# One tuned attention-and-FFN kernel on one core: hidden tiles of the bias moved between engines, and VectorE's work in a late attention step put in another order

## The chip, the core and the metric

The kernel runs on one core of a Trainium2 chip. The metric is the device time of one execution in microseconds (us), as the median of several executions. The core has a matrix engine (TensorE, PE in the profile) and three engines for other work: VectorE (DVE), ScalarE (ACT) and GpSimd (POOL). SyncE (SP) issues the DMA transfers. Each engine runs its own queue of instructions in order; engines wait for each other by semaphores.

## The reference

Three stages follow each other. The first is attention with a relative bias that a tiny network makes out of the two positions, the second and third are two feed-forward networks over 1152 tokens.

```
scores = q @ k.T / sqrt(64)                       # 2 batches, 8 heads, 576 x 576, head size 64
x      = log1p(|i - j|) / log1p(max(i, 1))
bias   = relu(x * w1 + b1) @ w2                   # 32 hidden units, one column for each head
attn   = softmax(scores + bias);  out = attn @ v
h = x @ w_in;  g = h * sigmoid(1.702 h);  x = g @ w_out          # 512 -> 2048 -> 512
h = x @ w_in;  g = P(h) / (Q(h) + 1e-6);  x = g @ w_out          # P cubic, Q with |h| and h*h
```

## The kernel before

**The bias** is made in 36 beats, `i` = 0 to 35, each for 16 rows of positions. A beat `i` emits three things, in this order: `bias_out(i-3)`, which scales a finished PSUM result into the SBUF tile `st` (line L137 on ScalarE, L135 on VectorE in three beats), makes the mirrored part of it by a copy called the image (L139 ScalarE, L141 VectorE, L143 GpSimd) and stores it to DRAM; `bias_matmul(i-2)` (L117), which multiplies four hidden tiles by `w2` into a PSUM tile (`wide`, of which there are two that the attention scores also use, or `narrow`, of which there is one); and `bias_hidden(i)`, which makes the four hidden tiles of its rows, `max(u, -b)` or the same as a relu, in the buffer `room`. The tiles are 304 to 576 columns wide. Hidden tiles 0 and 1 are VectorE's (L98), tile 2 is GpSimd's (L93), tile 3 is ScalarE's (L91), but in the beats 4, 5, 6, 11, 16, 21, 24, 26, 30 and 33 it is VectorE's. VectorE reads `u` from SBUF (`bc`) where a tile is wider than 512 columns, which is so in the beats 0 to 7, and from a copy of it in PSUM (`up`) elsewhere. `room` has three buffers that the beats use in turn, two from beat 30 on.

**The attention** has 40 steps. A step handles 128 queries of two heads, or 64 queries of two heads as one block ("single-head" in VectorE's eyes: one pass over 576 columns); the latter has `qc` 4. On PE a step issues the transpose of a late piece of step s-3 (`tails`, L279, into the first scores tile), the scores of step s (L213, twelve matmuls in a two-head step, the heads in turn), some products with v (L338, L341) and the transposes of step s-3 (L306). On VectorE it issues, for each head, one instruction that adds the bias and takes the minimum (L234, followed by a short read of its accumulator), the sum plus a small number of step s-1 (L221), the reciprocal of it (L248), and the copy of the transposed late piece out of PSUM (`PTt`, L288, or two small ones, L292). ScalarE then makes the exponentials (L238). GpSimd scales the exponentials of step s-1 by the reciprocal (L251, one for each head) and then their last 64 columns (`ptl`, L255 or L257), which `tails` reads three steps after the step that made them. In the steps 19, 23, 28, 33 and 37 a piece of the first FFN's weight conversion is done as well: L409, L414, L416 on VectorE, L413 and L425 on ScalarE, L426 on GpSimd.

The beats of the bias are spread ahead of and between steps 0 to 11. The order of work inside a step comes from a list of two-letter names that the program walks: `xa` and `xb` are L234 of the first and of the second head with their exponentials, `su` is L221, `no` is the reciprocal and GpSimd's scaling, `to` is the `PTt` copy, `cv` the weight conversion, `vo`, `vl`, `kh`, `kl`, `qh`, `ql`, `ea`, `eb`, `pv` and `tr` are other pieces. Steps 0 to 11 have one list, the later steps another. An instruction's place in its engine's queue is its place in the program.

**The FFNs** follow. Their first chunk waits for the converted weights; after that PE is nearly always at work.

Of the kernel before, what the change touches and what calls it, by code (L numbers as in the profile page):

```python
# [29 lines left out]
TLAG = 3  # L30

FIRST = (19, 19, 21, 26, 30, 30, 39, 39, 39, 41, 41)


C_T, C_M, C_NI, C_W1, C_B1, C_W2 = 0, 576, 720, 756, 757, 758
# [11 lines left out]
class Attention:  # L47
# [34 lines left out]
    def bias_hidden(self, r):  # L82
        nc, bc = self.nc, self.bc
        i = self.rows.index(r)
        tiles = []
        for g in range(4):
            h = self.room[i % 3 if i < 30 else i % 2][g][:, 0:max(16 * r + 16, S - 16 * r)]
            u = bc[:, C_T:C_T + h.shape[1]]
            k = 4 * r + g
            if g == 3 and i not in (4, 5, 6, 11, 16, 21, 24, 26, 30, 33):  # L90
                nc.scalar.activation(out=h, in_=u, func=AF.Relu, bias=self.bm[:, k:k + 1])  # L91
            elif g == 2:
                nc.gpsimd.tensor_scalar(out=h, in0=u, scalar1=3.0e38, scalar2=self.nbm[:, k:k + 1],  # L93
                                        op0=ALU.min, op1=ALU.max)
            else:
                if h.shape[1] <= 512:
                    u = self.up[:, 0:h.shape[1]]
                nc.vector.tensor_scalar(out=h, in0=u, scalar1=self.nbm[:, k:k + 1], scalar2=None, op0=ALU.max)  # L98
            tiles.append(h)
        self.hid[r] = tiles  # L100
# [20 lines left out]
    def bias_out(self, r):  # L121
        nc = self.nc
        st = self.bp.tile([128, BW], F32, tag="st", name="st", bufs=4)
        c = int(self.rows.index(r) not in (4, 5, 6, 11, 16, 21, 24, 26, 30, 33))
        ps, left = self.bps.pop(r), 16 * r + 15
        n = ps.shape[1]

        if r < 18:
            side, other, image = st[:, left:], st[:, 0:left], st[:, 2 * left:left:-1]
        else:  # L130
            side, other, image = st[:, 0:n], st[:, n:], st[:, left - 1:left - (S - 16 * r):-1]
        i = self.rows.index(r)
        scale, bias = self.bc[:, C_NI + r:C_NI + r + 1], self.corr[:, c:c + 1]
        if i in (19, 28, 29):
            nc.vector.tensor_scalar(out=side, in0=ps, scalar1=scale, scalar2=bias, op0=ALU.mult, op1=ALU.add)  # L135
        else:
            nc.scalar.activation(out=side, in_=ps, func=AF.Identity, scale=scale, bias=bias)  # L137
        if i in (2, 3, 4, 7, 10, 13, 15, 18, 19, 21, 23, 24, 31, 32, 35):
            nc.scalar.copy(other, image)  # L139
        elif i in (3, 8, 10, 12, 14, 15, 24, 29):  # L140
            nc.vector.tensor_copy(other, image)  # L141
        else:
            nc.gpsimd.tensor_scalar(out=other, in0=image, scalar1=1.0, scalar2=1.0, op0=ALU.mult, op1=ALU.mult)  # L143
        n = H * BR + 1
        rows = self.bd[128 * BR * r:128 * BR * r + 16 * n].rearrange("(i n) -> i n", n=n)[:, 0:H * BR]
        nc.sync.dma_start(rows.rearrange("i (h j) -> i h j", h=H)[:, :, 0:BW], st[:])
# [373 lines left out]
def attention_moe_moe(tc, t):  # L520
# [82 lines left out]
    def conv(now=True):  # L603
        M.conv(nj[0])
        nj[0] += 1
        if now:
            M.split()

    pv, hq, due = [], [], []
    A.pv = pv  # L610
    g, nh = {}, 0
    for s in range(n + TLAG + 2):
        prep = []
        while s <= 10 and beats[0] < FIRST[s]:
            beat()
        if s < n:
            hp, b, qc = A.steps[s]
            pb = 2 * hp + b
            i = QORDER.index(qc)
# [25 lines left out]
        if s == 10:  # L645
            A.xp.release()
            A.xp = new(name="xt", bufs=1, space=PSUM, reuse_waits="tile")
        for piece in (('ea', 'to', 'qh', 'eb', 'ql', 'kh', 'xa', 'su', 'cv', 'pv', 'tr', 'xb', 'no', 'vo', 'kl', 'vl') if s < 12 else ('ea', 'vo', 'su', 'pv', 'eb', 'qh', 'ql', 'kh', 'xa', 'tr', 'no', 'to', 'xb', 'vl', 'cv', 'kl')):
            if piece == 'ea':
                A.evacuate(0)  # L650
            elif piece == 'eb':
                A.evacuate(1)
            elif piece == 'su':
                A.sums(s - 1)
            elif piece == 'to':
                A.tails_out(s - TLAG)
            elif piece == 'vo':
                A.values_out()
            elif piece == 'vl':
                A.values_lo()  # L660
            elif piece == 'qh':
                for x, part in prep:
                    if part == 0:
                        A.q_high(x)
            elif piece == 'kh':
                for x, part in prep:
                    if part == 1:
                        A.k_high(x)
            elif piece == 'kl':
                for x, part in prep:  # L670
                    if part == 2:
                        A.k_low(x)
            elif piece == 'ql':
                for x, part in prep:
                    if part in (1, 3):
                        A.q_low(x, 320 if part == 1 else 0, 640 if part == 1 else 320)
            elif piece == 'xa':
                A.exps(s, 0)
            elif piece == 'xb':
                A.exps(s, 1)  # L680
            elif piece == 'no':
                A.normalise(s - 1)
            elif piece == 'tr':
                A.transposes(s - TLAG)
            elif piece == 'pv':
                for _ in range(5 if s >= n or len(pv) > 5 else ((3,2,2,2),)[0][(4,0,1,2,3).index(pv[0][1])-1] if pv and pv[0][1] != 3 and False else 3 if pv and pv[0][1] == 4 else 2):
                    if pv and s >= 10:
                        A.values(*pv.pop(0))
                if s == n + TLAG + 1 and 1:
                    A.values_out()  # L690
                    A.values_lo()
            elif piece == 'cv':
                for _ in range(n - s in (3, 7, 12, 17, 21) if s < n else (0, 3, 0, 2, 0)[s - n]):
                    conv()
        if s < n:
# [3 lines left out]
            if s:  # L699
                h, o, c = A.steps[s - 1]  # L700
# [50 lines left out]
    for n in range(nh, len(seq) + L2):  # L751
        l, c, k = seq[n] if n < len(seq) else (2, 0, 0)
# [21 lines left out]
        if n >= N1 + RLAG:  # L774
            r = M.rational(hq.pop(0) if hq else None)
# [3 lines left out]
        while todo and n >= todo[0] + LAG[seq[todo[0]][0]]:  # L779
            m = todo.pop(0)  # L780
            l, c, k = seq[m]
# [100 lines left out]
```

## Time and profile before

| what | value |
|---|---|
| time, median of 3 runs | 629.62 us (629.3 to 630.92) |
| time of the profiled execution | 630.97 us |
| its span, first to last instruction | 629.2 us |
| PE busy | 591.3 us, 94% of the span |
| VectorE, ScalarE, GpSimd busy | 430.6, 439.6 and 375.0 us |
| mean granted clock of PE | 0.987 |

The shares are means over stages with different limits, so that they name no bound by themselves: the first 75 us (the bias), some 120 us of attention and the two FFNs have to be read apart. 1.8 us of the profiled execution lie outside its span. The profiled execution is 0.2% above the median of the three runs.

### The profile page before, as it was taken

How to read it: one execution, taken by the hardware profiler on the slowest of the kernel's cores; microseconds unless marked ns; L12 is line 12 of the kernel's file. 1: busy time of each engine (PE TensorE's matmuls, PEld its weight loads, DVE VectorE, ACT ScalarE, POOL GpSimd, SP SyncE). 2: the span in 40 equal slices, each digit the busy share in tenths (PEclk: the TensorE clock that was granted, in tenths of full speed). 3: DMA queues.
4: the chain of work that ended last, by engine and by line, in shares of the span. 5: the costliest groups of instructions: out<-in, count | busy, mean ns of one | idle time of the engine just before them, and what ended most of it. 6: DMA issues, size and time to landing. Idle time of an engine off the chain costs nothing.

```text
span 629.2 us, 10515 instructions
## 1 busy us (share of the span) xinstructions
PE 591.3 (94%) x3562; PEld 488.2 (78%) x3562; DVE 430.6 (68%) x905; ACT 439.6 (70%) x913; POOL 375.0 (60%) x450
## 2 busy tenths in 40 slices
PE   6886999999999898899999999997999999999997
PEld 2233466666666798899999988997998999999995
DVE  7988856787786788832112688877787776666663
ACT  6876777877887666633223566678888988878884
POOL 5846565666765576742222477766667766655663
PEclk9988999999999999999999999998999999999999
DMA  5688762914323476620000266630100100001001
GB/s 178 199 244 266 213 232 65 341 54 163 123 89 126 138 206 203 216 83 1 1 1 33 89 213 202 207 129 2 33 2 1 50 2 1 1 1 51 1 2 50
DMA packets 23910, 66.23 MB, mean 105 GB/s; under 512 B 2480, under 2 KB 3376, under 8 KB 23856
## 3 DMA queue, kind: packets, MB, share of 16 engines
q1 hardware_dynamic: 23712, 65.43, 32.3%
q8 instruction: 28, 0.46, 0.3%
q14 instruction: 26, 0.21, 0.1%
q10 hardware_dynamic: 144, 0.13, 0.1%
HBM read 52.30 MB, written 13.25 MB: 104 GB/s over the span
## 4 chain that ended last, share of the span: by engine, by line
PE 36%; DVE 14%; ACT 13%; issue 2%; POOL 0%; DVEq 0%; ACTq 0%
PE hps L437 18%; PE acc L516 12%; PE acc L509 6%; DVE tmp L409 5%; ACT up L413 3%; ACT w L425 3%; DVE sg L456 2%; DVE tmp L416 2%; DVE top L414 2%; ACT sg L455 2%; ACT ra L480 1%; ACT sq L472 1%; ACT ra L479 1%; ACT ra L478 1%; ACT ra L475 1%
## 5 line engine op out<-in xcount | busy, mean ns | idle before, releaser
L437 PE MATMUL hps<-xhi,w 128*128 128x384 f32 x768 | 153.5, 341 | 14.5 <-DVE sg L456 9.8
L437 PEld LDWEIGHTS hps<-xhi,w 128*128 128x128 f32 x768 | 136.1, 189 | 24.8 <-DVE sg L456 15.6
L426 POOL TENSOR_TENSOR w<-tmp,w 128x512 fp32r<-128x512 f32 x64 | 82.4, 1288 | 43.0 <-ACT w L425 36.9
L449 POOL TENSOR_TENSOR glo<-sg,ghi 128x384 fp32r<-128x384 f32 x48 | 48.8, 1017 | 64.4 <-PE acc L509 45.0
L437 PE MATMUL hps<-xlo,w 128*128 128x384 f32 x384 | 82.1, 334 | 0.0
L251 POOL TENSOR_SCALAR p<-p,mn 128x512 f32<-128x512 f32 x72 | 51.8, 730 | 46.1 <-DVE PTt L288 23.0
L238 ACT ACTIVATE p<-p,mn 128x576 f32<-128x576 f32 x72 | 55.8, 776 | 30.4 <-DVE mn L234 17.9
L509 PE MATMUL acc<-ghi,w 128*128 128x384 f32 x384 | 76.7, 334 | 0.0
L516 PE MATMUL acc<-w,ghi 128*128 128x512 f32 x288 | 75.8, 393 | 0.0
L456 DVE TENSOR_TENSOR sg<-hps,sg 128x384 f32<-128x384 f32 x48 | 26.8, 557 | 65.6 <-ACT sg L455 65.6
L437 PEld LDWEIGHTS hps<-xlo,w 128*128 128x128 f32 x384 | 68.2, 188 | 0.0
L489 POOL TENSOR_SCALAR ra<-ra,small 128x384 f32<-128x384 f32 x48 | 28.2, 587 | 66.2 <-ACT ra L478 66.2
L509 PEld LDWEIGHTS acc<-ghi,w 128*128 128x128 f32 x384 | 67.5, 188 | 0.0
L234 DVE CUSTOM_DVE_ANT_0 p<-wide,bt 128x576 f32<-128x576 f32 x72 | 54.1, 752 | 14.7 <-PE wide L213 10.5
L413 ACT ACTIVATE up<-raw 128x512 int32<-128x512 uint32 x59 | 38.0, 643 | 36.5 <-DVE tmp L409 33.7
L516 PEld LDWEIGHTS acc<-w,ghi 128*128 128x128 f32 x288 | 53.4, 188 | 8.6
L488 DVE TENSOR_TENSOR ra<-ra,hps 128x384 f32<-128x384 f32 x48 | 26.6, 555 | 37.4 <-ACT ra L480 37.3
L446 ACT CAST ghi<-sg 128x384 fp32r<-128x384 f32 x48 | 24.7, 514 | 38.2 <-DVE sg L456 19.8
L491 POOL TENSOR_TENSOR ra<-ra 128x384 f32<-128x384 f32 x48 | 48.7, 1015 | 4.0
L213 PE MATMUL wide<-k,q 64*128 64x288 f32 (+1 forms) x432 | 48.9, 319 | 2.1 <-ACT st L137 1.2
L449 POOL TENSOR_TENSOR glo<-ra,ghi 128x384 fp32r<-128x384 f32 x48 | 48.8, 1017 | 2.7 <-PE acc L516 2.0
L213 PEld LDWEIGHTS wide<-k,q 64*128 64x128 f32 (+1 forms) x432 | 36.9, 191 | 11.4 <-DVE mn L234 3.4
(93 smaller groups left out, 1173.8 us busy)
## 6 DMA issues: line engine op xcount, KB each, us to landing
raw<-win SPq DMA_DIRECT2D x32, 512.0 KB, 3.6
raw<-wout SPq DMA_DIRECT2D x32, 512.0 KB, 3.7
bias_all<-st SPq DMA_DIRECT2D x36, 295.5 KB, 3.4
bt<-bias_all SPq DMA_DIRECT2D x16, 576.0 KB, 5.6
qk<-qk SPq DMA_DIRECT2D x7, 608.0 KB, 6.3
v<-v SPq DMA_DIRECT2D x8, 320.0 KB, 4.6
out<-o SPq DMA_DIRECT2D x8, 256.0 KB, 2.2
bt<-bias_all SPq DMA_DIRECT2D x8, 144.0 KB, 3.6
```

What stands on the lines that cost most here:

```text
L213: nc.tensor.matmul(ps[:, half, 0:288], q[p, x, 128 * qc:128 * qc + 128], k[p, y, 288 * half:288 * half + 288], start=(i == 0), stop=(i == ...
L234: nc.vector.tensor_tensor_reduce(out=pv.rearrange("p (x j) -> p x j", x=2), in0=ps[:, :, 0:288], in1=self.bt[qc][:, a, :].rearrange("p (x ...
L238: nc.scalar.activation(out=pv, in_=pv, func=AF.Exp, bias=mn[:, a:a + 1], scale=-1.0, accum_out=mn[:, 2 + a:3 + a])
L251: nc.gpsimd.tensor_scalar(out=p[:, a, 0:512], in0=p[:, a, 0:512], scalar1=r, scalar2=1.0, op0=ALU.mult, op1=ALU.mult)
L413: nc.scalar.activation(out=self.up[j].bitcast(I32), in_=lo, func=AF.Copy, scale=2.0 ** -29)
L426: nc.gpsimd.tensor_tensor(out=w[:, 2 * o + 1, :], in0=val, in1=w[:, 2 * o, :].bitcast(F32), op=ALU.subtract)
L437: nc.tensor.matmul(ps[:, 0:CH], w[:, wi, 128 * d:128 * d + 128], xx[:, d, :], start=(i == 0 and d == 0), stop=(i == 2 and d == 3))
L449: nc.gpsimd.tensor_tensor(out=glo[:], in0=g, in1=ghi[:].bitcast(F32), op=ALU.subtract)
L456: nc.vector.tensor_tensor(out=sg[:], in0=h, in1=sg[:], op=ALU.mult)
L491: nc.gpsimd.tensor_tensor(out=t0[0][:], in0=t0[0][:], in1=t0[1][:], op=ALU.add)
L509: nc.tensor.matmul(acc[e][:, 0:CH], w[:, wi, 128 * e:128 * e + 128], g[gi][:], start=(k == 0 and i == 0), stop=(k == NF - 1 and i == 2))
L516: nc.tensor.matmul(acc[e][:], g[gi][:, 128 * e:128 * e + 128], w[:, wi, :], start=(k == 0 and i == 0), stop=(k == NF - 1 and i == 2))
```

## The change

Two things are changed. In `bias_hidden` the list of ten beats is replaced by `GP3`, seven beats, and in these hidden tile 3 goes to GpSimd; in the other beats it is ScalarE's. So it leaves VectorE in the beats 5, 11, 16, 21, 24, 30 and 33 for GpSimd, and in the beats 4, 6 and 26 for ScalarE. The list of VectorE's image copies loses 3, 10, 15, 24 and 29; of these the first four are in ScalarE's list, which is asked first, so that only the copy of i = 29 has another engine now, GpSimd.

In the list of pieces for steps from 12 on, `to` comes ahead of `pv`, and `su` and `no` come behind `xb`.

```
+GP3 = (5, 11, 16, 21, 24, 30, 33)
...
-            if g == 3 and i not in (4, 5, 6, 11, 16, 21, 24, 26, 30, 33):
+            if g == 3 and i not in GP3:
                 nc.scalar.activation(out=h, in_=u, func=AF.Relu, bias=self.bm[:, k:k + 1])
-            elif g == 2:
+            elif g >= 2:
                 nc.gpsimd.tensor_scalar(out=h, in0=u, scalar1=3.0e38, scalar2=self.nbm[:, k:k + 1],
...
-        c = int(self.rows.index(r) not in (4, 5, 6, 11, 16, 21, 24, 26, 30, 33))
+        c = int(self.rows.index(r) not in GP3)
...
         if i in (2, 3, 4, 7, 10, 13, 15, 18, 19, 21, 23, 24, 31, 32, 35):
             nc.scalar.copy(other, image)
-        elif i in (3, 8, 10, 12, 14, 15, 24, 29):
+        elif i in (8, 12, 14):
             nc.vector.tensor_copy(other, image)
...
-  ... else ('ea', 'vo', 'su', 'pv', 'eb', 'qh', 'ql', 'kh', 'xa', 'tr', 'no', 'to', 'xb', 'vl', 'cv', 'kl')):
+  ... else ('ea', 'vo', 'to', 'pv', 'eb', 'qh', 'ql', 'kh', 'xa', 'tr', 'xb', 'su', 'no', 'vl', 'cv', 'kl')):
```

The lines of the kernel after are three higher than before (L98 becomes L101, L234 becomes L237 and so on). VectorE's queue over the beats 2 to 7 of the bias, before and then after; `room` is a hidden tile, `bc` the SBUF source:

```order
L98 TENSOR_SCALAR room<-bc,nbm 128x560 x2
L98 TENSOR_SCALAR room<-bc,nbm 128x576 x5
L98 TENSOR_SCALAR room<-bc,nbm 128x560 x3
L98 TENSOR_SCALAR room<-bc,nbm 128x544 x3
L98 TENSOR_SCALAR room<-bc,nbm 128x528 x2
```

```order
L101 TENSOR_SCALAR room<-bc,nbm 128x560 x2
L101 TENSOR_SCALAR room<-bc,nbm 128x576 x4
L101 TENSOR_SCALAR room<-bc,nbm 128x560 x2
L101 TENSOR_SCALAR room<-bc,nbm 128x544 x2
L101 TENSOR_SCALAR room<-bc,nbm 128x528 x2
```

Three of fifteen hidden tiles are gone there. GpSimd's queue at the same place, before and then after (`q` is the split of the queries, `st` an image copy):

```order
L143 TENSOR_SCALAR st<-st 128x47
L93 TENSOR_SCALAR room<-bc,nbm 128x576
L93 TENSOR_SCALAR room<-bc,nbm 128x560
L186 TENSOR_TENSOR q<-qk,q 128x320
L93 TENSOR_SCALAR room<-bc,nbm 128x544
L93 TENSOR_SCALAR room<-bc,nbm 128x528
```

```order
L146 TENSOR_SCALAR st<-st 128x47
L96 TENSOR_SCALAR room<-bc,nbm 128x576
L96 TENSOR_SCALAR room<-bc,nbm 128x560 x2
L189 TENSOR_TENSOR q<-qk,q 128x320
L96 TENSOR_SCALAR room<-bc,nbm 128x544
L96 TENSOR_SCALAR room<-bc,nbm 128x528
```

One tile of beat 5 came in. VectorE's queue in the attention steps 23 (with weight conversion) and 24, before and then after; the row `mn 128x1` is the accumulator's read, `p` the scores with bias:

```order
L234 ISA p,mn<-wide,bt 128x576
L234 ISA mn 128x1
L248 RECIPROCAL mn<-mn 128x2
L292 COPY PTt<-wide 64x64 x2
L234 ISA p,mn<-wide,bt 128x576
L234 ISA mn 128x1
L409 ISA tmp<-raw,tmp 128x1024
L414 TENSOR_SCALAR tmp<-raw 128x512
L416 SCALAR_TENSOR_TENSOR tmp<-raw,tmp 128x512
L221 TENSOR_SCALAR mn<-mn 128x2
L234 ISA p,mn<-wide,bt 128x576
```

```order
L295 COPY PTt<-wide 64x64 x2
L237 ISA p,mn<-wide,bt 128x576
L237 ISA mn 128x1
L237 ISA p,mn<-wide,bt 128x576
L237 ISA mn 128x1
L224 TENSOR_SCALAR mn<-mn 128x2
L251 RECIPROCAL mn<-mn 128x2
L412 ISA tmp<-raw,tmp 128x1024
L417 TENSOR_SCALAR tmp<-raw 128x512
L419 SCALAR_TENSOR_TENSOR tmp<-raw,tmp 128x512
L291 COPY PTt<-wide 128x128
L237 ISA p,mn<-wide,bt 128x576
```

The copy stands ahead of the first read of scores, the reciprocal behind the second, and the sum of step 24 is no longer between the conversion of step 23 and the scores of step 24. The queues of PE and SP are the same as before; ScalarE has three more hidden tiles and nothing else that differs.

## Rows read from the trace of the kernel before

**Rows 1.** Stretches: length; busy PE, PEld, DVE, ACT, POOL; clock; DMA

```profile
25.00:30.00 5.00, 4.16 (x28) 0.86 (x24) 5.00 (x9) 4.97 (x11) 4.07 (x7) 1.00 0.84 265
...
50.00:55.00 5.00, 4.37 (x32) 1.62 (x36) 3.32 (x11) 4.14 (x9) 2.54 (x5) 0.66 0.97 332
...
95.00:192.00 97.00, 93.78 (x735) 62.90 (x732) 72.91 (x233) 78.40 (x185) 64.74 (x94) 1.00 0.39 135
```

**Rows 2.** VectorE's timeline, bias: start, length, line, count, [idle before <-releaser]

```profile
8.47 9.82 DVE L98 TENSOR_SCALAR room<-bc,nbm 128x560 f32<-128x560 f32 x15
...
41.09 0.76 DVE L234 CUSTOM_DVE_ANT_0 p<-wide,bt 128x576 f32<-128x576 f32 x1 [1.53 <-PE wide L213]
...
43.29 5.82 DVE L98 TENSOR_SCALAR room<-up,nbm 128x304 f32<-128x304 f32 x12
...
53.91 4.01 DVE L98 TENSOR_SCALAR room<-up,nbm 128x400 f32<-128x400 f32 x7 [1.03 <-PE narrow L117]
...
66.60 5.76 DVE L98 TENSOR_SCALAR room<-up,nbm 128x464 f32<-128x464 f32 x9
```

**Rows 3.** PE's timeline, bias

```profile
50.40 1.35 PE L117 MATMUL wide<-room,bc 128*32 128x336 f32 x8 [2.42 <-DVE mn L221]
...
59.23 0.88 PE L117 MATMUL wide<-room,bc 128*32 128x400 f32 x8 [2.37 <-DVE mn L221]
```

**Rows 4.** Lines L98 and L93: durations in ns, least, median, most

```profile
L98 DVE TENSOR_SCALAR room<-up,nbm x63: 516/633/740, 18.9 to 71.6; 128x480 f32<-128x480 f32 x5, 128x464 f32<-128x464 f32 x5, 128x432 f32<-128x432 f32 x5, 128x384 f32<-128x384 f32 x5
L98 DVE TENSOR_SCALAR room<-bc,nbm x19: 481/935/1111, 5.0 to 17.8; 128x544 f32<-128x544 f32 x5, 128x560 f32<-128x560 f32 x5, 128x576 f32<-128x576 f32 x5, 128x528 f32<-128x528 f32 x4
...
L93 POOL TENSOR_SCALAR room<-bc,nbm x36: 513/628/1365, 5.0 to 70.3; 128x528 f32<-128x528 f32 x2, 128x544 f32<-128x544 f32 x2, 128x560 f32<-128x560 f32 x2, 128x576 f32<-128x576 f32 x2
```

**Rows 5.** ScalarE's timeline, bias, scaling of the second 576-wide result

```profile
14.46 0.83 ACT L137 ACTIVATE st<-wide,corr,bc 128x576 f32<-128x576 f32 x1 [0.63 <-POOL room L93]
```

**Rows 6.** VectorE's timeline, attention step 8: copy ahead of the first read

```profile
80.24 0.29 DVE L288 COPY PTt<-wide 128x128 f32<-128x128 f32 x1 [0.36 <-PE wide L213]
80.45 0.75 DVE L234 CUSTOM_DVE_ANT_0 p<-wide,bt 128x576 f32<-128x576 f32 x1
```

**Rows 7.** VectorE's timeline, weight conversion of step 23, and step 24

```profile
135.07 1.03 DVE L409 CUSTOM_DVE_ANT_0 tmp<-raw,tmp 128x1024 uint16<-128x1024 uint16 x1
...
137.29 1.24 DVE L221 TENSOR_SCALAR mn<-mn 128x2 f32<-128x2 f32 x1
138.44 0.74 DVE L234 CUSTOM_DVE_ANT_0 p<-wide,bt 128x576 f32<-128x576 f32 x1
...
139.11 0.15 DVE L248 RECIPROCAL mn<-mn 128x2 f32<-128x2 f32 x1
139.19 0.26 DVE L288 COPY PTt<-wide 128x128 f32<-128x128 f32 x1
139.38 0.74 DVE L234 CUSTOM_DVE_ANT_0 p<-wide,bt 128x576 f32<-128x576 f32 x1
```

**Rows 8.** PE's timeline, steps 23 to 26

```profile
134.89 1.37 PE L213 MATMUL wide<-k,q 64*128 64x288 f32 x12
...
139.60 0.30 PE L279 MATMUL wide<-cst,ptl 128*128 128x128 f32 x1 [0.67 <-DVE PTt L288]
...
142.56 0.27 PE L279 MATMUL wide<-cst,ptl 128*128 128x128 f32 x1
```

**Rows 9.** GpSimd's timeline, steps 24 to 37

```profile
137.21 1.28 POOL L426 TENSOR_TENSOR w<-tmp,w 128x512 fp32r<-128x512 f32 x1 [0.85 <-ACT w L425]
...
139.47 1.36 POOL L251 TENSOR_SCALAR p<-p,mn 128x512 f32<-128x512 f32 x2 [0.97 <-DVE PTt L288]
140.80 0.40 POOL L255 TENSOR_TENSOR ptl<-p,mn 128x128 f32<-128x128 f32 x1
...
183.49 2.08 POOL L251 TENSOR_SCALAR p<-p,mn 128x512 f32<-128x512 f32 x2 [1.79 <-DVE PTt L288]
185.54 0.83 POOL L255 TENSOR_TENSOR ptl<-p,mn 128x128 f32<-128x128 f32 x1
```

More of the change, by code (lines that the diff above doesn't have):

```diff
@@ L647, in attention_moe_moe @@
             A.xp = new(name="xt", bufs=1, space=PSUM, reuse_waits="tile")
-        for piece in (('ea', 'to', 'qh', 'eb', 'ql', 'kh', 'xa', 'su', 'cv', 'pv', 'tr', 'xb', 'no', 'vo', 'kl', 'vl') if s < 12 else ('ea', 'vo', 'su', 'pv', 'eb', 'qh', 'ql', 'kh', 'xa', 'tr', 'no', 'to', 'xb', 'vl', 'cv', 'kl')):
+        for piece in (('ea', 'to', 'qh', 'eb', 'ql', 'kh', 'xa', 'su', 'cv', 'pv', 'tr', 'xb', 'no', 'vo', 'kl', 'vl') if s < 12 else ('ea', 'vo', 'to', 'pv', 'eb', 'qh', 'ql', 'kh', 'xa', 'tr', 'xb', 'su', 'no', 'vl', 'cv', 'kl')):
             if piece == 'ea':
```

## The prediction

> **What bounds the kernel now.** I read the kernel by stretches first, since its busy shares are a mean over stages [rows 1]. Over 95 to 192 us, the attention, PE is busy for 93.78 of 97 us, so only the few waits of PE are to be had there. The FFNs behind it are not touched. In the bias it is another engine: VectorE runs one unbroken row of hidden tiles after another, 15 tiles in 9.82 us from 8.47 on, 12 in 5.82 us from 43.29 on, 7 in 4.01 us from 53.91 on, 9 in 5.76 us from 66.60 on [rows 2], and PE waits for it: its idle time of 2.42 us ahead of 50.40 and of 2.37 us ahead of 59.23 both end with VectorE's instructions of the attention step that stands behind such a row [rows 3]. So what leaves these rows can count in full, as long as the engine that gets it has room. From 25 to 30 us that is doubtful: ScalarE is busy for 4.97 of 5 us there, VectorE for 5.00 [rows 1].
>
> **The bias, part by part.** Ten hidden tiles and one image copy leave VectorE: the beats 4, 6 and 26 give to ScalarE, the others to GpSimd. (The words of the change speak of fifteen; four of the five image copies were ScalarE's already.)
>
> Beats 4, 5 and 6: these are three of the 15 tiles that took 9.82 us, 0.65 us each [rows 2], 1.96 us if VectorE alone sets the pace. Against it speaks that ScalarE waited 0.63 us there, and what it waited for ends with a hidden tile of GpSimd [rows 5]; GpSimd now gets one more tile, ScalarE two. The low bound is 0, the high bound 1.96; I take 0.8, under the middle, because of that wait.
>
> Beat 11: one tile, 0.6 us by the same kind of row, in or just ahead of the stretch in which ScalarE has no room [rows 1]. I take 0, high bound 0.6.
>
> Beat 16: one tile, its cost by the nearest rows 4.01/7 = 0.57 or 5.82/12 = 0.49 us; 0.5.
>
> Beat 21: its tile stands ahead of VectorE's wait of 1.53 us for scores at 41.09 [rows 2], so the wait only grows: 0.
>
> Beats 24 and 26: two of the 12 tiles ahead of 49.1 us, 2 x 5.82/12 = 0.97 us. PE waits 2.42 us for the end of that row [rows 3], more than is taken, so all of it counts.
>
> Beat 30: one of the 7 tiles, 4.01/7 = 0.57 us; PE's wait of 2.37 us covers it [rows 3], all of it counts.
>
> Beat 33 and the image of beat 29: 5.76/9 = 0.64 us for the tile and about as much for the copy leave VectorE in the last row [rows 2]. Both go to GpSimd, whose own tiles there take the median of 0.63 us [rows 4], as long as VectorE's, and which has to finish the tiles of the last beats as well. Bounds -0.4 (GpSimd ends later than VectorE did) and 1.3; I take 0.
>
> The sum is 0.8 + 0.5 + 0.97 + 0.57 = 2.84 us, bounds about 0.7 (the early beats bring nothing, the rows that PE waits for bring half) and 4.7. Nothing that I read behind the bias absorbs it: the steps that follow wait for tiles and loads that move along.
>
> A row and a rule on GpSimd. VectorE's hidden tiles from SBUF take 481 to 1111 ns, with a median of 935, those from PSUM 516 to 740 with 633, although the former are only little wider [rows 4]; the ones from SBUF are stretched while GpSimd works. The Trainium skill, "SBUF — State Buffer", section "Who interferes with whom", says that a VectorE instruction in a two-port mode, or with two SBUF inputs, shares a port pair with GpSimd, and that whoever comes first blocks the other for its whole instruction. The rows agree as far as they go. By that rule the tile of beat 5 would save VectorE nothing, since GpSimd's instruction shuts out what VectorE wins; the early term would be that of the beats 4 and 6 alone, at most 1.3 us. It speaks against the move of beat 5 and not against the rest, since the later tiles are read from PSUM.
>
> **The attention, part by part.** In a two-head step VectorE waits for the last scores of the first head; call that moment T. Before, the order is read, reciprocal, copy, read: 138.44, 139.11, 139.19, 139.38 [rows 7], so the second read ends at T + 0.94 + 0.74 = T + 1.68 and the first scores tile is free with the copy at T + 1.01. After, the copy comes first. What it costs is shown by the steps up to 11, which have it first already: it doesn't start before the scores are done (idle until 80.24, released by the scores), and the read follows 0.21 us later [rows 6]. So T + 0.21 + 0.75 = T + 0.96 frees the first tile, and the second read ends 0.75 later at T + 1.71. Ordinary steps gain nothing: 0.05 earlier for the one tile, 0.03 later for the other.
>
> The three conversion steps that lie between two-head steps (23, 28, 33) do gain. There the sum of step 24 stands behind the conversion and takes 1.24 us instead of the 0.15 of a like instruction, while GpSimd runs L426 from 137.21 to 138.49; the read follows at 138.44, though the scores had ended at 134.89 + 1.37 = 136.26 [rows 7 to 9]. So the copy comes late, and PE stands 0.67 us ahead of 139.60 until it has come [rows 8]. After the change, sum and reciprocal run before the conversion, which so starts some 0.2 us later, and the 1.24 us are no longer in the way: the first read comes some 0.8 us earlier and PE's gap of 0.67 goes, at most 3 x 0.67 = 2.0 us. What may be late next is GpSimd's scaling, which starts later now and falls on the conversion: there it takes 2.08 + 0.83 us, as at 183.49, where it otherwise takes 1.36 + 0.40 [rows 9]. I take 0.5 each, 1.5 us, bounds 0 and 2.0.
>
> The price of the new order is the reciprocal: at T + 0.67 before, now behind both reads and the sum, at about T + 1.71 + 0.1 = T + 1.8, so 1.1 us later. GpSimd's scaling waits for it, and `tails` three steps on waits for `ptl`. After step 23 that ended at 140.80 + 0.40 = 141.20, and PE used it at 142.56 [rows 8, 9]: 1.36 us of room, of which 0.25 are left. The trace has three such places; elsewhere the room is larger or the step has one head, where the reciprocal follows the one read, at T + 0.96 + 0.1, and moves by only some 0.4. I take 0.5 us of loss for this in all, bounds 0 and 3.
>
> The attention brings 1.5 - 0.5 = 1.0 us, bounds -1.5 and 2.0.
>
> **The sum.** 630.97 us of the profiled execution less 2.84 and 1.0 is 627.1; the median of the runs is 0.9979 of that execution, so 625.8 us.
>
> **The rivals.**
> A. *ScalarE or GpSimd becomes the bound of the bias.* The wait at 14.46 and ScalarE's 4.97 of 5 us speak for it, the long waits of PE for VectorE at 50 and 59 us against it [rows 1, 3, 5]. The bias brings its low bound, 0.7: 630.97 - 0.7 - 1.0 = 629.3, by the median 627.9 us.
> B. *PE's clock.* From 50 to 55 us the mean granted clock is 0.66 [rows 1], a part of it at the lower level of 1.2 GHz, and it falls right behind PE's wait of 2.42 us [rows 3]. If the shorter waits leave PE at 2.4 GHz here and behind the second wait, more comes back than VectorE gave: of those 5 us, 0.34 x 5 = 1.7 us of full speed are missing, and I count that once: 630.97 - 3.84 - 1.7 = 625.4, by the median 624.1 us. For it speaks that the waits shrink to some 1.4 and 1.8 us; against it that 1.4 us is still a long wait.
> C. *The copy is hidden under the scores,* and both reads follow each other from T on. Then the second read ends at T + 1.5, 0.2 earlier in each of some 22 steps, up to 4.4 us: 630.97 - 3.84 - 4.4 = 622.7, by the median 621.4 us. The copy that starts only with the end of the scores speaks against it [rows 6].
> D. *GpSimd's scaling ends the attention steps: slower.* Its scaling starts 1.1 us later, and where VectorE's reads or the conversion stretch it as at 183.49, it takes 2.91 instead of 1.76 us [rows 9]: 2.25 us later against 1.36 of room, 0.9 us for each step. It decides from the point where the stretching holds in ordinary steps and not only in those with conversion: with nine steps 8.0 us, against the bias's 2.84: 630.97 - 2.84 + 8.0 = 636.1. With half as many it is 632.1, by the median 630.8 to 634.8; I take 632.5 as its middle. The rule of the Trainium skill on the shared ports, named above, is what would do this; the reads take one input from PSUM and one from SBUF, and scaling beside them took 1.36 us [rows 7, 9], so this trace doesn't bear it out for ordinary steps.
> E. *It does not do what it says:* eleven instructions leave VectorE, where they leave it the beats wait for the scores or a PSUM tile anyway, and the attention gives 0: 629.6 us. The waits of 1.53 and 1.03 us for PE speak for it [rows 2], the two waits of PE for VectorE against it [rows 3].
>
> **How the numbers follow.** Chances: the forecast 0.42, A 0.17, B 0.15, C 0.04, D 0.12, E 0.10. The forecast's own range is 624 to 627.7. The range for 8 in 10 takes in A, B and E and the near half of D, and leaves out C and the far half of D: 622.0 to 631.0. A measurement of this kernel can tell 0.3%, 1.9 us, from no change: faster is below 627.7, slower above 631.5. Faster: most of the forecast, 0.38, B and C, 0.19, and under half of A, 0.08: 0.65. Slower: most of D, 0.1. Same: the rest, 0.25.
>
> **What would show it right or wrong.** In the bias: VectorE's tiles ahead of the third two-head step should be ten instead of twelve, and that step's first read some 2.3 us earlier than 49.48, its successor some 2.8 us earlier; PE's waits of 2.4 us should be 1.4 and 1.8. If ScalarE or GpSimd are what PE waits for at these places, A holds. In the attention: copy and first read 0.2 us apart at T, no sum of 1.2 us behind the conversion, no wait of PE on a VectorE copy there; a wait of `tails` for `ptl` would show D. I am wrong if the first read at 35.6 us has not moved, if the copy starts before the scores end (C), or if the stages behind the attention change by more than they are moved.

## The result

The kernel after takes 623.31 us (median of 4 runs, 621.84 to 624.12) against 629.46 us (median of 4, 629.12 to 630.92) before: 0.9895 of the time, interval 0.987 to 0.992. That is 6.15 us less; 3.8 were forecast. The time lies in the stated range (622.0 to 631.0) and below the forecast's own range (624 to 627.7).

The profiled execution of the kernel after took 621.84 us (span 620.1), which is the lowest of its four times, and that of before 630.97, just above the highest of its four. So the two traces are 9.1 us apart, some 3 us more than the medians. Where that comes from is seen by comparing the start of the same work in the two traces:

| place | before, us | after, us | earlier by |
|---|---|---|---|
| first read of scores, step 0 | 35.64 | 33.15 | 2.49 |
| step 2 | 41.09 | 38.95 | 2.14 |
| step 3 | 49.48 | 46.32 | 3.16 |
| step 4 | 58.31 | 54.25 | 4.06 |
| scores on PE, step 12 | 93.60 | 88.99 | 4.61 |
| step 24 | 134.89 | 129.78 | 5.11 |
| step 25 | 139.66 | 133.53 | 6.13 |
| step 39 | 188.37 | 179.98 | 8.39 |
| end | 629.2 | 620.1 | 9.1 |

The bias gave 4.6 us in this pair of traces, the late attention steps 3.8, the FFNs, which are the same code, 0.7. The last number says nothing: from step 39 to the end the traces of all kernels below take between 440.1 and 442.5 us. The first is too large, since the trace of before has a slow bias. Four other traces have the bias as before (order_only, sum_only, copy_only and split_late, below), two others as after (bias_only and sum_behind_conv); in them the same places are

| place | bias as before, 5 traces, us | bias as after, 3 traces, us | difference of the middle ones |
|---|---|---|---|
| first read of scores, step 0 | 34.75 to 35.64 | 33.15 to 33.69 | 1.9 |
| step 2 | 39.72 to 41.21 | 38.84 to 39.28 | 1.6 |
| from step 2 to step 3 | 8.21 to 8.39 | 7.37 in all | 1.0 |
| from step 3 to step 4 | 7.56 to 7.60, before 8.83 | 7.87 to 7.93 | -0.4 |
| scores on PE, step 12 | 91.08 to 93.60 | 88.99 to 90.69 | 1.8 |

So the bias part of the change is worth about 1.8 us up to step 12, and the rest of the 4.6 is a matter of these two executions. The stretches of the bias after (columns as in [rows 1]) show one reason:

```profile
40.00:45.00 5.00, 3.83 (x37) 1.32 (x30) 5.00 (x13) 4.97 (x12) 3.65 (x8) 1.00 0.72 211
45.00:50.00 5.00, 3.52 (x40) 1.60 (x38) 4.78 (x14) 4.34 (x11) 3.89 (x7) 1.00 0.88 245
50.00:55.00 5.00, 2.49 (x21) 1.29 (x21) 4.07 (x10) 4.26 (x8) 3.48 (x7) 1.00 1.00 356
55.00:60.00 5.00, 4.84 (x45) 2.84 (x49) 4.55 (x14) 3.54 (x8) 4.22 (x8) 1.00 0.77 237
```

The granted clock of PE is 1.00 throughout, where 50 to 55 us had 0.66 before [rows 1] and 0.95 to 1.00 in the four other traces with the old bias. The other three runs of the kernel after had mean clocks of 0.989 to 0.992 against 0.997 of this one, and were 1.0 to 2.3 us longer. A part of the 9.1 us is thus this execution's clock and not the change.

In the bias VectorE's rows are shorter by the tiles that left, and new waits have come in, one of them for a transfer (`bt`, the bias read back from DRAM); this is VectorE's timeline after, columns as in [rows 2]:

```profile
8.35 8.58 DVE L101 TENSOR_SCALAR room<-bc,nbm 128x560 f32<-128x560 f32 x12
...
38.95 0.76 DVE L237 CUSTOM_DVE_ANT_0 p<-wide,bt 128x576 f32<-128x576 f32 x1 [2.04 <-DMA bt<-bias_all]
...
41.05 4.83 DVE L101 TENSOR_SCALAR room<-up,nbm 128x304 f32<-128x304 f32 x10
...
49.34 2.29 DVE L101 TENSOR_SCALAR room<-up,nbm 128x400 f32<-128x400 f32 x4 [0.20 <-PE narrow L120]
51.85 1.24 DVE L101 TENSOR_SCALAR room<-up,nbm 128x432 f32<-128x432 f32 x2 [0.22 <-PE narrow L120]
53.76 0.46 DVE L295 COPY PTt<-wide 64x64 f32<-64x64 f32 x2 [0.67 <-PE wide L216]
```

Twelve tiles take 8.58 us where fifteen took 9.82, ten take 4.83 where twelve took 5.82 [rows 2]. The three early tiles thus brought 1.24 us and not three times the mean of 0.65: of the fifteen, eight took 0.48 to 0.52 us and seven 0.94 to 1.11, of the twelve, five and seven, so that three quick ones are gone, each of which held the row for some 0.41 us until the next one started. The seven tiles from beat 28 to 30, an unbroken 4.01 us before, are now six with waits of 0.22 and 0.67 us among and behind them: there VectorE no longer sets the pace. On PE, the two waits of [rows 3] are now

```profile
47.23 0.77 PE L120 MATMUL wide<-room,bc 128*32 128x336 f32 x8 [1.42 <-DVE mn L237]
...
50.98 0.85 PE L120 MATMUL narrow<-room,bc 128*32 128x384 f32 x8 [1.04 <-ACT st L140]
...
55.16 0.88 PE L120 MATMUL wide<-room,bc 128*32 128x400 f32 x8 [1.31 <-DVE mn L224]
```

1.42 and 1.31 us (1.4 and 1.8 were expected), and between them stands a wait of 1.04 us for ScalarE.

In the attention the conversion step 23 and step 24 answer to [rows 7, 8]. VectorE's timeline after (the first two rows are the copy and the first read of step 22), then PE's:

```profile
123.77 0.29 DVE L291 COPY PTt<-wide 128x128 f32<-128x128 f32 x1 [0.38 <-PE wide L216]
123.97 0.74 DVE L237 CUSTOM_DVE_ANT_0 p<-wide,bt 128x576 f32<-128x576 f32 x1
...
130.01 0.17 DVE L251 RECIPROCAL mn<-mn 128x2 f32<-128x2 f32 x1
130.09 0.67 DVE L412 CUSTOM_DVE_ANT_0 tmp<-raw,tmp 128x1024 uint16<-128x1024 uint16 x1
...
132.03 0.28 DVE L291 COPY PTt<-wide 128x128 f32<-128x128 f32 x1
132.23 0.74 DVE L237 CUSTOM_DVE_ANT_0 p<-wide,bt 128x576 f32<-128x576 f32 x1
...
132.91 0.74 DVE L237 CUSTOM_DVE_ANT_0 p<-wide,bt 128x576 f32<-128x576 f32 x1
...
133.58 0.72 DVE L224 TENSOR_SCALAR mn<-mn 128x2 f32<-128x2 f32 x1
```

```profile
129.78 1.22 PE L216 MATMUL wide<-k,q 64*128 64x288 f32 x12
...
132.57 1.09 PE L309 MATMUL pt<-cst,p 128*128 128x128 f32 x8
133.50 0.27 PE L282 MATMUL wide<-cst,ptl 128*128 128x128 f32 x1
133.53 1.04 PE L216 MATMUL wide<-k,q 128*128 128x288 f32 x6
...
136.49 0.33 PE L282 MATMUL wide<-cst,ptl 128*128 128x128 f32 x1
```

These rows of PE's timeline before belong beside them:

```profile
127.33 0.30 PE L279 MATMUL wide<-cst,ptl 128*128 128x128 f32 x1 [0.26 <-DVE PTt L288]
...
137.83 1.10 PE L306 MATMUL pt<-cst,p 128*128 128x128 f32 x8
...
145.13 0.30 PE L279 MATMUL wide<-cst,ptl 128*128 128x128 f32 x1 [0.28 <-DVE PTt L288]
```

The first read comes 1.23 us after the end of its scores (129.78 + 1.22 = 131.00), before it was 2.18 us. PE's wait of 0.67 us on the copy is gone, and from the scores of step 24 to those of step 25 it is 3.75 us instead of 4.77. Of these 1.02 us, 0.84 lie ahead of `tails`, which comes 0.93 us after the start of the transposes instead of 1.77, and 0.15 in the scores of step 24 (1.22 us, before 1.37).

The sum still is slowed by L429 of GpSimd (0.72 us), but stands behind both reads, where PE's scores do not wait for it. The reciprocal waits for it, and with that GpSimd's scaling. GpSimd's timeline after:

```profile
130.37 2.30 POOL L254 TENSOR_SCALAR p<-p,mn 128x512 f32<-128x512 f32 x2 [1.61 <-ACT p L241]
132.64 0.40 POOL L258 TENSOR_TENSOR ptl<-p,mn 128x128 f32<-128x128 f32 x1
133.00 1.28 POOL L429 TENSOR_TENSOR w<-tmp,w 128x512 fp32r<-128x512 f32 x1
134.70 1.37 POOL L254 TENSOR_SCALAR p<-p,mn 128x512 f32<-128x512 f32 x2 [0.42 <-PE wide L216]
136.03 0.40 POOL L258 TENSOR_TENSOR ptl<-p,mn 128x128 f32<-128x128 f32 x1
```

This `ptl` is done at 136.43, and the `tails` that reads it, that of step 26, starts at 136.49: the room of 1.36 us is used up. The steps 25, 30 and 35 are 0.12, 0.10 and 0.09 us longer than before, scores to scores.

### The profile page after: what moved, and what is told of

The parts are those of the page before. It is cut to its first block, busy times and chain, and to the rows that moved or that the text cites. A ratio compares the mean times of both kernels' runs of the same rounds, so it can differ in the third digit from the quotient of the medians.

```text
span 620.1 us, 10492 instructions
## 1 busy us (share of the span) xinstructions
PE 585.4 (94%) x3562; PEld 486.8 (79%) x3562; DVE 422.9 (68%) x894; ACT 439.2 (71%) x916; POOL 379.7 (61%) x458
## 4 chain that ended last, share of the span: by engine, by line
PE 37%; DVE 14%; ACT 13%; issue 2%; POOL 0%; DVEq 0%; ACTq 0%
PE hps L440 18%; PE acc L519 12%; PE acc L512 6%; DVE tmp L412 5%; ACT up L416 3%; ACT w L428 3%; DVE sg L459 2%; DVE tmp L419 2%; DVE top L417 2%; ACT sg L458 2%; ACT ra L483 1%; ACT sq L475 1%; ACT ra L482 1%; ACT ra L478 1%; DVE ra L495 1%
## 5 line engine op out<-in xcount | busy, mean ns | idle before, releaser
L429 POOL TENSOR_TENSOR w<-tmp,w 128x512 fp32r<-128x512 f32 x64 | 82.5, 1288 | 39.0 <-ACT w L428 32.9
L254 POOL TENSOR_SCALAR p<-p,mn 128x512 f32<-128x512 f32 x72 | 55.2, 777 | 41.6 <-ACT p L241 26.1
L237 DVE CUSTOM_DVE_ANT_0 p<-wide,bt 128x576 f32<-128x576 f32 x72 | 52.2, 749 | 2.5 <-DMA bt<-bias_all 2.0
L216 PE MATMUL wide<-k,q 64*128 64x288 f32 (+1 forms) x432 | 47.3, 311 | 2.4 <-ACT st L140 2.1
L458 ACT ACTIVATE sg<-hps 128x384 f32<-128x384 f32 x48 | 23.4, 487 | 30.7 <-PE hps L440 30.7
```

What stands on the lines that cost most here:

```text
L216: nc.tensor.matmul(ps[:, half, 0:288], q[p, x, 128 * qc:128 * qc + 128], k[p, y, 288 * half:288 * half + 288], start=(i == 0), stop=(i == ...
L237: nc.vector.tensor_tensor_reduce(out=pv.rearrange("p (x j) -> p x j", x=2), in0=ps[:, :, 0:288], in1=self.bt[qc][:, a, :].rearrange("p (x ...
L254: nc.gpsimd.tensor_scalar(out=p[:, a, 0:512], in0=p[:, a, 0:512], scalar1=r, scalar2=1.0, op0=ALU.mult, op1=ALU.mult)
L429: nc.gpsimd.tensor_tensor(out=w[:, 2 * o + 1, :], in0=val, in1=w[:, 2 * o, :].bitcast(F32), op=ALU.subtract)
```

## How the runs are compared

Times of one kernel differ by up to 5 us between runs, and go with the mean granted clock of the run. A straight line through the timed runs of all kernels, with one slope and a level for each kernel, has 0.27 us for 0.001 of clock (two runs whose records show 0.94 to 0.95 without a longer time are left out). The table gives the median, the measured ratio to before with its interval, and the level at a clock of 0.988, which is the median clock of the kernel before, as a difference to before.

| kernel | median, us (runs) | ratio, interval | difference at clock 0.988, us |
|---|---|---|---|
| after | 623.31 (4) | 0.9895, 0.987 to 0.992 | -6.0 |
| bias_only | 627.64 (11) | 0.9954, 0.9936 to 0.9972 | -2.3 |
| order_only | 626.09 (7) | 0.9943, 0.9922 to 0.9964 | -4.1 |
| copy_only | 625.77 (6) | 0.9936, 0.9916 to 0.9956 | -4.0 |
| sum_only | 628.30 (12) | 0.9976, 0.996 to 0.9992 | -2.2 |
| split_late | 628.69 (12) | 0.9972, 0.9955 to 0.9989 | -1.6 |
| sum_behind_conv | 631.02 (12) | 1.0013, 1.0001 to 1.0026 | +1.4 |
| early_five | 629.04 (12) | 0.9974, 0.9963 to 0.9986 | -1.4 |
| late_five | 628.77 (12) | 0.9981, 0.9969 to 0.9993 | -0.7 |
| beat30_back | 622.15 (4) | 0.9879, 0.9864 to 0.9895 | -6.1 |
| early_order | 623.15 (4) | 0.9886, 0.9871 to 0.9901 | -6.1 |
| six_moves | 624.90 (6) | 0.993, 0.9914 to 0.9946 | -5.3 |
| scores_twice | 629.84 (11) | 0.999, 0.9977 to 1.0003 | +0.4 |

The kernel before had medians of 629.46 to 630.30 us beside these. The last column is worked out, not measured, and good to about half a microsecond. The runs come from several chips; a level of its own for each chip would move no entry by more than that.

## Experiments on the two parts

**bias_only**: the change in the bias, steps in the old order.

```
-... else ('ea', 'vo', 'to', 'pv', 'eb', 'qh', 'ql', 'kh', 'xa', 'tr', 'xb', 'su', 'no', 'vl', 'cv', 'kl')):
+... else ('ea', 'vo', 'su', 'pv', 'eb', 'qh', 'ql', 'kh', 'xa', 'tr', 'no', 'to', 'xb', 'vl', 'cv', 'kl')):
```

> The bias part of the change alone; the steps keep the order of before. Theory (the two parts add up, the late order brings about 3.5 us): the first scores read of step 0 at about 33.2 us, step 11's scores 4 to 4.6 us earlier than before, and the attention from step 12 to 39 as long as before; 629.5 less about 3 = 626 to 626.8 us. Rival (the bias brings nearly all, the rest is the clock): 623 to 624.5 us.

**order_only**: the reverse, the new order in the kernel before.

> The new order of the late steps alone; the bias as before. Theory: step 12 starts where it did, each of the three conversion steps 23, 28 and 33 is 1.0 us shorter from scores to scores, the others within 0.2 us; about 3.5 us in all, 625.7 to 626.5 us. Rival (the order brings at most the 1 us that was predicted): 628 to 629 us.

Measured: the bias alone 2.0 us by the medians of one chip (629.65 to 627.64) or 2.9 by the ratio, the order alone 3.6 by either; 6.4 together at equal clock, against 6.0 of the whole change. So the parts add up, and the larger one is the order of the steps. In the trace of bias_only the steps from 12 to 39 are as long as before to 0.03 us; in that of order_only the steps 24, 29 and 34, each counted from its scores to the next and each behind the conversion of the step before it, are 1.02, 1.03 and 1.02 us shorter, which is what the kernel after shows.

## Experiments on the order of the steps

**sum_only** and **copy_only** make half of the reordering each, on the kernel before:

```
-('ea', 'vo', 'su', 'pv', 'eb', 'qh', 'ql', 'kh', 'xa', 'tr', 'no', 'to', 'xb', 'vl', 'cv', 'kl')
+('ea', 'vo', 'pv', 'eb', 'qh', 'ql', 'kh', 'xa', 'tr', 'to', 'xb', 'su', 'no', 'vl', 'cv', 'kl')      # sum_only
+('ea', 'vo', 'su', 'to', 'pv', 'eb', 'qh', 'ql', 'kh', 'xa', 'tr', 'no', 'xb', 'vl', 'cv', 'kl')      # copy_only
```

> Of the new order only this: sum and reciprocal stand behind the second read, the copy stays between the two reads; the bias as before. Theory (the gain comes from the sum that no longer stands behind the conversion, where GpSimd holds it up): the whole gain of the new order, 1.0 us in each of the three conversion steps, 625.7 to 626.5 us. Rival (the two reads back to back are what brings the gain): within 0.5 us of the kernel before, 629.0 to 630 us.

> Of the new order only this: the copy stands ahead of the first read; sum and reciprocal stay where they were before, the sum ahead of the copy; the bias as before. Theory: the sum still waits 1.2 us behind the conversion, the copy still waits for the scores, so nothing: 629 to 630 us. Rival (the copy is what gains, since tails waits for it): 627 us or less.

This did not come out as the theory had it. copy_only brings as much as the whole new order (-4.0 us at equal clock), sum_only about half (-2.2). But the steps 24, 29 and 34 are shorter in both, by 0.92 us each in sum_only and by 0.94 to 0.98 in copy_only, so that the difference between the two does not lie there. Where it lies stays open. The trace of sum_only ran at a granted clock of 0.95 nearly from end to end: most of its other steps are 0.03 to 0.09 us longer than before, and the steps 13, 19, 21, 26, 31 and 36, in which order_only gains, are 0.05 to 0.08 us shorter. Against its own slower rest it gains in them what order_only does, so that this trace shows no step in which sum_only loses. So moving the sum out of the way is one way to get the 1 us, and there is another. VectorE's timeline of copy_only shows it:

```profile
134.64 0.36 DVE L221 TENSOR_SCALAR mn<-mn 128x2 f32<-128x2 f32 x1
134.91 0.28 DVE L288 COPY PTt<-wide 128x128 f32<-128x128 f32 x1
135.11 0.74 DVE L234 CUSTOM_DVE_ANT_0 p<-wide,bt 128x576 f32<-128x576 f32 x1
```

The sum stands where it stood, behind the conversion, but takes 0.36 us and not 1.24. GpSimd's timeline of the same kernel has the reason:

```profile
132.13 2.04 POOL L251 TENSOR_SCALAR p<-p,mn 128x512 f32<-128x512 f32 x2 [1.24 <-DVE mn L248]
134.14 0.83 POOL L255 TENSOR_TENSOR ptl<-p,mn 128x128 f32<-128x128 f32 x1
134.94 1.27 POOL L426 TENSOR_TENSOR w<-tmp,w 128x512 fp32r<-128x512 f32 x1
```

GpSimd's scaling falls on the conversion and is stretched (2.04 us, where it took 1.36 in [rows 9]), so L426 begins only at 134.94, behind the sum. Before, L426 began at 137.21 and the sum at 137.29 [rows 7, 9].

**split_late** tries that collision by itself: the order of before, but L425 and L426 are issued one step later.

```
+    late = [False]
...
             elif piece == 'cv':
+                if late[0]:
+                    M.split()
+                late[0] = False
                 for _ in range(n - s in (3, 7, 12, 17, 21) if s < n else (0, 3, 0, 2, 0)[s - n]):
-                    conv()
+                    conv(s >= n)
+                    late[0] = s < n
```

> The kernel before, steps in the old order, with one difference: in the attention the last two instructions of a piece of weight conversion (L425 on ScalarE, L426 on GpSimd) are issued one step later, behind GpSimd's scaling. Theory (what costs is the sum that collides with L426 behind the conversion): the sum of the step behind a conversion falls from 1.24 to below 0.4 us, the three conversion steps are about 0.9 us shorter each, 2.5 to 3 us in all, 626.8 us. Rival (the position of copy and sum as such costs, not the collision): within 0.7 us of the kernel before.

The sum behind the conversion takes 0.16 us, and PE no longer waits there; VectorE's timeline of split_late:

```profile
135.84 0.16 DVE L221 TENSOR_SCALAR mn<-mn 128x2 f32<-128x2 f32 x1
135.91 0.75 DVE L234 CUSTOM_DVE_ANT_0 p<-wide,bt 128x576 f32<-128x576 f32 x1
```

Each of the three steps is 0.86 us shorter, as expected, and the step behind it 0.28 us longer, which was not expected; 1.8 us are left of the 2.5 to 3. With sum and reads in the old order, taking L426 away from the sum thus brings 0.86 of the 1.02 us. The collision is the cause of PE's wait. The scores of step 24 keep their 1.37 us here; only the new orders shorten them (1.22 us in order_only, 1.29 in copy_only, 1.26 in sum_only).

**sum_behind_conv** is the kernel after with sum and reciprocal at the end of the step, behind the conversion.

```
-... 'xa', 'tr', 'xb', 'su', 'no', 'vl', 'cv', 'kl')
+... 'xa', 'tr', 'xb', 'vl', 'cv', 'kl', 'su', 'no')
```

> The kernel after, but sum and reciprocal stand at the end of a step's VectorE work, behind the weight conversion; copy and two reads in front as in the kernel after. Theory: the sum collides with GpSimd or makes its scaling late, the three conversion steps lose up to 1 us each against the kernel after, 625 to 626.5 us. Rival (GpSimd's scaling has room enough, and the copy in front is what counts): within 0.7 us of the kernel after.

It is worse than expected: 631.02 us, 7.4 us above the kernel after at equal clock and, by its ratio, 0.1% slower than before. The copy is in front as in the kernel after, so the copy's place is not enough. PE's timeline and GpSimd's:

```profile
135.81 0.33 PE L282 MATMUL wide<-cst,ptl 128*128 128x128 f32 x1 [1.45 <-POOL ptl L258]
```

```profile
132.78 1.28 POOL L429 TENSOR_TENSOR w<-tmp,w 128x512 fp32r<-128x512 f32 x1 [3.00 <-DVE PTt L291]
134.03 1.36 POOL L254 TENSOR_SCALAR p<-p,mn 128x512 f32<-128x512 f32 x2
135.36 0.40 POOL L258 TENSOR_TENSOR ptl<-p,mn 128x128 f32<-128x128 f32 x1
```

The scaling stands behind L429 in GpSimd's queue here, `ptl` is done at 135.76, and `tails` waits 1.45 us for it. This is the mechanism of rival D, made by another order. In the kernel after no such wait is among PE's own; PE's weight loads wait 0.7 us in all for `ptl`, in two places. The kernel after has the reciprocal late enough to have the sum out of the reads' way and, but for the 0.1 us of each of the steps 25, 30 and 35, early enough for GpSimd.

**early_order** applies the same to the steps 0 to 11 of the kernel after, where the sum still stands between the reads.

```
-('ea', 'to', 'qh', 'eb', 'ql', 'kh', 'xa', 'su', 'cv', 'pv', 'tr', 'xb', 'no', 'vo', 'kl', 'vl')
+('ea', 'to', 'qh', 'eb', 'ql', 'kh', 'xa', 'cv', 'pv', 'tr', 'xb', 'su', 'no', 'vo', 'kl', 'vl')
```

> The kernel after, with the sum behind the second read in the steps 0 to 11 as well; the copy is in front there already. Theory: the sums between the reads of the steps 3, 4 and 5, which beside GpSimd's hidden tiles took 0.36, 0.19 and 0.47 us in the kernel after, are out of the way, about 0.1 to 0.35 us each, 0.5 us in all: 622.8 us. Rival (the later reciprocal makes GpSimd's scaling late in the steps 5 to 7, whose pieces are used within 0.2 us): slower by 0.5 to 2 us.

623.15 us, the same as the kernel after to within what can be told. Neither the gain nor the loss is seen.

## Experiments on the bias

**early_five** and **late_five** give half of the moves each, in the old order of steps. `DV3` holds the beats whose hidden tile 3 stays with VectorE, `GP3` those in which it goes to GpSimd. The cuts are against the kernel before; the image copy of beat 29 stays with VectorE in early_five and goes to GpSimd in late_five:

```
+GP3 = (5, 11, 16)                   # early_five;  late_five: (21, 24, 30, 33)
+DV3 = (21, 24, 26, 30, 33)          # early_five;  late_five: (4, 5, 6, 11, 16)
...
-            if g == 3 and i not in (4, 5, 6, 11, 16, 21, 24, 26, 30, 33):
+            if g == 3 and i not in GP3 + DV3:
...
-            elif g == 2:
+            elif g == 2 or (g == 3 and i in GP3):
```

> The bias moves of the beats 4, 5, 6, 11 and 16 alone; all else as before. Theory (the prediction's own terms 0.8 and 0.5): 1.3 us, 628.3 us, with the first read of step 0 at 34.3 us or earlier. Rival (VectorE alone sets the pace, each tile counts): 2.5 to 3 us, 626.9 us, step 0 at 33.1 us.

> The bias moves of the beats 21, 24, 26, 30 and 33 and of the image of beat 29 alone; all else as before. Theory (0.97 and 0.57): 1.5 us, 628.1 us. Rival (the late tiles bring nothing, since GpSimd or ScalarE end the beats then): within 0.4 us of the kernel before, and the whole gain of the bias lies in the early beats.

By the medians 1.3 and 1.5 us, by the ratios 1.6 and 1.2, at equal clock 1.4 and 0.7: together 2.1 to 2.8, as bias_only. In the trace of early_five the first read of step 0 came at 33.07 us, 2.57 earlier than in that of before (1.7 to 2.5 than in the others with the old bias), as the rival had it, and yet the runs as a whole kept only some 1.5 of it.

**beat30_back**: the kernel after with the tile of beat 30 on VectorE again (`DV3 = (30,)`, `GP3` without 30).

> The kernel after, but the third hidden tile of beat 30 is VectorE's again. Theory (VectorE waits for ScalarE and PE there now, 0.20, 0.22 and 0.67 us, so that this move brought next to nothing): within 0.3 us of the kernel after. Rival (the prediction's term, 0.57 us, holds): 0.5 to 0.6 us slower than the kernel after.

622.15 us; at equal clock the same as the kernel after. The rival's 0.57 us are not there. VectorE's timeline shows why:

```profile
52.02 1.82 DVE L102 TENSOR_SCALAR room<-up,nbm 128x432 f32<-128x432 f32 x3 [0.23 <-PE narrow L121]
54.02 0.46 DVE L296 COPY PTt<-wide 64x64 f32<-64x64 f32 x2 [0.19 <-PE wide L217]
```

The third tile fills the wait: 0.19 us ahead of the copy instead of 0.67. The copy starts 0.26 us later than in the kernel after, and 0.15 of that this trace was behind already at the first read of step 3 (46.47 against 46.32).

**six_moves**: the kernel after, with the five moves that were counted or found to bring nothing undone.

```
-GP3 = (5, 11, 16, 21, 24, 30, 33)
+GP3 = (5, 16, 24)
+DV3 = (11, 21, 30, 33)
...
-        elif i in (8, 12, 14):
+        elif i in (8, 12, 14, 29):
```

> The kernel after, but with only six of its eleven moves in the bias: the hidden tiles of the beats 5, 16 and 24 on GpSimd and of 4, 6 and 26 on ScalarE. Those of 11, 21, 30 and 33 and the image of beat 29, which the prediction counted at nothing or which a run showed to bring nothing (beat 30), are VectorE's again. Theory (those terms are nothing): within 0.5 us of the kernel after, 622.8 to 623.8 us. Rival (two or more of the five count after all): 624.5 us or more.

624.90 us, in the rival's half by 0.4 us; at equal clock 0.75 above the kernel after, by the ratios 2.2. Its trace speaks the other way: with the clock at 1.00 all through the bias, as in the trace of after, the scores of step 12 come 0.6 us earlier than there (88.4 against 88.99), but three traces with one and the same bias code already differ by 1.7 us at this place (88.99 to 90.69), so that one trace can't decide it. Whether the five moves bring some tenths, or keep PE's clock up in more runs (median clock 0.9875 here, 0.9905 after), stays open.

**scores_twice**: the kernel before, with the scores of the steps 3 and 4 computed twice over, to fill PE's waits of 2.4 us.

```
-        for half in range(2):
+        for half in (0, 1, 0, 1) if s in (3, 4) else (0, 1):
```

> The kernel before, but PE computes the scores of the steps 3 and 4 twice over (the second time writes the same numbers again), which fills some 1.1 us of each of the two waits of 2.4 us in which VectorE still makes hidden tiles. Theory (the granted clock in this stretch depends on how long PE waits there): the runs' mean granted clock is higher, 0.992 or more in most, and the time 1 to 2.5 us lower although PE has more to do. Rival (the clock comes and goes with something else): clock and time as before, within 0.5 us, or longer where the repeated scores come too late.

The clock did go up: the median of the runs' mean clocks is 0.991 (11 runs) against 0.988 (15 runs), and in the profiled run it is 1.00 throughout the stretch:

```profile
45.00:50.00 5.00, 3.40 (x41) 2.24 (x41) 4.97 (x13) 3.06 (x7) 3.07 (x6) 1.00 0.87 231
50.00:55.00 5.00, 4.14 (x47) 1.93 (x41) 4.67 (x11) 4.95 (x12) 3.82 (x8) 1.00 0.98 339
55.00:60.00 5.00, 3.69 (x43) 2.55 (x40) 4.35 (x13) 4.04 (x9) 3.94 (x7) 1.00 0.95 298
```

These rows alone prove little, since the trace of order_only, without the repeated scores, has 1.00 from 40 to 55 us too (0.88 and 0.78 in the two stretches behind). And the time is only 0.1% lower, with an interval that includes 1. So over the runs the clock went up with more work in PE's waits, which is what the theory said of the clock, and the gain of 1 to 2.5 us in time is not there.

## Why the prediction came out as it did

*What bounds the kernel.* Right: VectorE's rows of hidden tiles set the pace of the bias up to step 3, and the attention is PE's. But the attention had more to give than PE's waits for VectorE's copy, 2.9 us in all before: it gave 3.8.

*The bias, 2.84 us.* The sum was near, 2.0 to 2.9 us in bias_only and 2.3 at equal clock, but by luck in part, since its terms erred in both directions. The early beats were put at 1.3 us; the middle traces have 1.9 at the first read of step 0, and 1.6 at step 2, where the scores, or in some traces a transfer of the bias table, ended last (2.04 us of waiting ahead of 38.95), and early_five as a whole kept 1.3 to 1.6. The term of beats 24 and 26, 0.97 us, shows in the traces: the way from step 2 to step 3 is 0.8 to 1.0 us shorter in every one with the bias of after. The term of beat 30, 0.57 us, was wrong: the step "PE's wait covers it, all of it counts" looked at PE's wait and not at who is late next on VectorE's side; by the rows that is the single `narrow` buffer behind ScalarE (1.04 us on PE). beat30_back showed the move to be nothing, and from step 3 to step 4 the bias of after takes 0.3 us longer than four of the five traces with the bias of before. Here rival A holds, for one row of tiles and not for all. (The high bound of 4.7 us is not the sum of the high bounds above it, which is 5.9; nothing else hangs on it.)

*Ordinary attention steps, nothing.* Right for the copy, wrong for the sum. The copy that comes first does wait for the scores, as the rows of step 8 had shown: in step 22 of the kernel after it starts at 123.77, released by the scores, and the read follows 0.20 us behind it, so that rival C is out, though its 4.4 us are near what the attention gave. But the steps 13, 14, 19, 21, 26, 31 and 36 gained 0.09 to 0.17 us where 0.05 was worked out, 1.0 us in all. Three of them, 21, 26 and 36, ended before with waits of PE for the copy of 0.26 to 0.29 us (at 127.33, 145.13 and 180.79), which the prediction does not count.

*The conversion steps, 1.5 us.* The mechanism was right, the size half of what it was: 1.02 us for each of the three steps, 3.1 in all. The bound of 0.67 for each was taken from PE's idle time ahead of `tails`; but from the start of the transposes `tails` came 0.84 us earlier, and the scores of the step were 0.15 us shorter. PE's waits ahead of single matmuls do not hold all that a stage loses. And the 0.17 that were taken off for GpSimd's late scaling were not lost: in the kernel after the scaling took 2.30 us there and `ptl` was done at 133.04, in time for the 133.50 of `tails`.

*The price of the late reciprocal, 0.5 us.* The mechanism was right and the price 0.3 us, about 0.1 in each of the steps 25, 30 and 35. In copy_only, which has the copy in front and the reciprocal in its old place, these steps are as long as before to 0.01 us. The prediction had the reciprocal, and `ptl` with it, 1.1 us later against 1.36 of room; counted from the first read, `ptl` was done 1.44 us later (138.44 to 141.20 before, 132.23 to 136.43 after), because the sum ahead of the reciprocal took 0.72 us beside L429 and not 0.1. sum_behind_conv shows what more of it costs. In all the attention gave 3.1 + 1.0 - 0.3 = 3.8 us, where 1.5 + 0 - 0.5 = 1.0 were forecast.

*The clock.* Rival B was counted at 1.7 us with a chance of 0.15. The median clock of the runs rose from 0.988 to 0.9905, which at 0.27 us for 0.001 is 0.7 us. That clock and time go together is shown by the runs; scores_twice doesn't show that a higher clock in the bias alone makes the kernel faster.

*Net.* 3.8 us were forecast; 6.0 at equal clock came: about 2.3 from the bias for 2.84, 3.8 from the attention for 1.0. The time lies in the stated range, but partly by luck: the range went down to 622 for rival B, and what took the time there was the attention, whose term was too small by 2.8 us.

## What to carry to other kernels

A small instruction between two that matter can cost eight times its own length if it meets a long instruction of another engine; look at the longest of its kind, not the median, and at what ran beside it. What such a step loses is read from the period of the bounding engine's work, scores to scores, and not from the idle time ahead of one of its instructions. And when a tile is moved off a pacing engine, ask for each place whether that engine will then wait: a tile taken from such a stretch can buy only a wait, as in the beats 28 to 30 here.

## What the hardware showed

VectorE's sum over two columns takes 0.15 to 0.17 us, 1.24 beside GpSimd's L426 before, 0.72 after, 0.16 with L426 moved away. Beside it, it ends when GpSimd's instruction ends: at 138.53 with L426 at 138.49, at 134.30 with L429 at 134.28. It goes the other way too: GpSimd's two scalings take 1.36 us, but 2.04 to 2.30 where VectorE's conversion runs beside them, and VectorE's first conversion instruction took 0.67 us where it started ahead of GpSimd's scaling (130.09 and 130.37) and 1.03 where it started at 135.07 beside a scaling that ran from 134.20 to 135.56. The Trainium skill, "SBUF — State Buffer", section "Who interferes with whom", describes such a lock between the two engines, held for a whole instruction; these numbers agree with it. The prediction named the rule for the hidden tiles, where by it the move of beat 5 would save nothing. The row of tiles became 1.24 us shorter, near the 1.3 that this allows; but three quick tiles less make as much, and the move was not tried alone, so that this stays open.
